# Attention into a top-1 mixture of experts: exponentials two steps behind, flips beside the sums, ranks behind them

## The chip, the core and the metric

One NeuronCore of a Trainium2 chip runs the kernel as one program. The metric is device time in microseconds (us), median of the runs shown. Five engines work side by side, each through its own queue in order: TensorE (PE, with weight loads as PEld), VectorE (DVE), ScalarE (ACT), GpSimd (POOL) and SyncE (SP, which only issues transfers here). Matmul results land in PSUM, everything else lies in SBUF.

## The reference

Attention over 8 batches, 12 heads, 448 positions and 64 features, with a tanh cap on the scores, then a router that picks one of 8 experts for each of the 3584 tokens, then that expert's two-layer network:

```python
scores = cap * np.tanh((q @ k.T / 8) / cap)
attn = softmax(scores)                 # over the keys
x = (attn @ v) -> tokens x 768
logits = x @ w_gate + modality_bias[modality_id]
e = argmax(logits); gate = softmax(logits)[e]
out[token] = gate * (relu(x @ w1[e]) @ w2[e])
```

## The kernel before

The 12 heads of a batch are 3 **units** of 4 heads, so there are 24 units `d`. A unit has 7 **steps** of 64 keys; step `n = 7 d + s` of 168 handles 64 keys against all 448 queries for the unit's 4 heads. Softmax needs no maximum, since the cap bounds the scores.

A step is this. PE makes scores: 4 matmuls (`scores`, L489) into one of two PSUM buffers `sc`. ACT takes a tanh of 128x896 into `pt` (L494). After each odd step ACT takes one exponential over the pair of steps, 128x1792 in place (L497). DVE adds the step's `pt` into the unit's `tot` (`add`, L510). PE multiplies an older step's `pt` with the values (`weigh`, L522) into the one PSUM buffer `xT`, which DVE copies out at a unit's end (`keep`, L529, "the values' copy"). In text below T(n) is the tanh of step n and E the exponential of a pair.

Everything is pinned to the order in which the loop over `n` writes it. `LAGS`, `PLAGS` say how many steps behind its scores a step's weigh stands; `BEHIND` does so for the additions. A step without a weigh is made up for by a step with two.

Every second unit, `sums2` (L556 ff.) sums over the keys for two units and multiplies the kept values with the gate weights: 8 matmuls into one PSUM bank `glog`, which DVE copies to `gl` (L567). `turn2` then flips `gl` with 4 transposes (`flip`, L552) into a bank `lt`, and DVE makes reciprocals (L580) and logits (`logits`, L603). When a batch is complete, `start_route` begins its route: a reduction (L250), the top expert, a small exponential on ACT (L269), running counts, then the **ranks**, two small matmuls (L290, L292) into a bank of their own, and row numbers (L296 to L303) by which POOL scatters the tokens into a map. `go_on` takes a route one stage further. The network of the experts (from about 306 us on) follows; it is not touched.

Of the kernel before, what the change touches and what calls it, by code (L numbers as in the profile page):

```python
# [80 lines left out]
PLAGS = (5, 5, 5, 4, 4, 4, 4)  # L81
# [4 lines left out]
class Program:  # L86
# [368 lines left out]
    def attention(self, firsts, rp, xp):  # L455
        tc, nc = self.tc, self.nc
        pe, pin, V = nc.tensor, self.pin, nc.vector
        with ExitStack() as st:
# [21 lines left out]

            def scores(n):

                d, s = divmod(n, STEPS)
                sc = ps_s.tile([128, 2, 512], F32, name="sc")
                for i in range(2):
                    kq = ring[(2 * d + i) % 4]
                    for j in range(2):
                        rows = slice(j * D, (j + 1) * D)
                        pin(pe.matmul(  # L489
                            sc[i * KB : (i + 1) * KB, j, :S], kq[rows, s * KB : (s + 1) * KB], kq[rows, S:QK],  # L490
                            start=True, stop=True,
                        ))
                slow = n // STEPS == SOON + 2 and 2 <= n % STEPS <= 5
                pin(nc.scalar.activation(weights(n), sc[:, :, :S], AF.Tanh, scale=self.isc if slow else self.iscr))  # L494
                if n % 2:
                    pt = pts[n // 2]
                    pin(nc.scalar.activation(pt, pt, AF.Exp, scale=self.cabsr))  # L497
# [33 lines left out]
            def sums(d, bank=None, copy=V.tensor_copy):  # L531
# [14 lines left out]
                gls[d] = xp.tile([128, S], F32, name="gl", bufs=2)  # L546
                pin(copy(gls[d], glog[:, :S]))

            def flip(gl, bank=None):
                bank = bank or self.ps_r.tile([128, 512], F32, name="lt", tag="small")  # L550
                for c in range(C):
                    pin(pe.transpose(bank[:CP, c * 128 : (c + 1) * 128], gl[:, c * CP : (c + 1) * CP], self.ident))  # L552
                return bank[:CP].rearrange("p (c g x) -> p c g x", c=C, g=4)

            def sums2(a, copy=V.tensor_copy):
# [10 lines left out]
                gls[a] = xp.tile([128, S], F32, name="gl", bufs=2)  # L566
                pin(copy(gls[a], glog[:, :S]))  # L567

# [7 lines left out]
            def turn2(a):  # L576

                lt = flip(gls.pop(a))
                for u in range(2):
                    pin(V.reciprocal(recs(a + u), lt[:, :, 2 * u : 2 * u + 2, GE : GE + 2]))  # L580
                    lts[a + u] = lt[:, :, 2 * u : 2 * u + 2]
# [48 lines left out]
            def start_route(b, firm=False):  # L630
                way = self.route(
                    b, lgs[b], pays[b], rp, self.ps_r, bank=(lambda: self.glog) if firm else None, firm=firm, late=firm
                )
                next(way)
                routing[:] = [way]
# [19 lines left out]
            for m in range(END):  # L655
                d, s = divmod(m, STEPS)
                due[min(m + (LAST if d == ND - 1 else PLAGS if d < PAIRED else LAGS[d % 2])[s], END)].append(m)
            added, held = 0, range(STEPS * (SOON + 2), STEPS * (SOON + 2) + 5)

            def more(n, count=0):  # L660
                nonlocal added
                while (n not in held or count > 0) and added <= n - BEHIND + (n >= END - STEPS):
# [5 lines left out]

            fetch(0)
            self.gate_weights()  # L670
            for n in range(END):
# [17 lines left out]
                if (s == 6 or s == 1) and d != SOON + 2:  # L689
                    go_on()  # L690
                if s == 4 and d % 2 and 3 <= d < PAIRED + 3:
                    turn2(d - 3)
                    go_on()
                    logits(d - 3)
                    logits(d - 2)
                if s == 4 and d % 2 == 0 and 2 <= d <= PAIRED:
                    sums2(d - 2)
                if (d, s) == (SOON + 1, 5):
                    sums(SOON)
                if s == 5 and d % 2 and 3 <= d < PAIRED + 2:  # L700
                    for u in (d - 3, d - 2):
                        if u % NU == NU - 1:
                            start_route(u // NU)
                if (d, s) == (SOON + 2, 2):
                    more(n, 2)
                for m in due[n]:
                    weigh(m)
                    if m % STEPS == STEPS - 1:
                        keep(m // STEPS)
                if s == 2 and d % NU == 2:  # L710
# [626 lines left out]
```

## Time and profile before

| | |
|---|---|
| median of 3 runs | 820.83 us (820.09 to 821.06) |
| profiled execution | 819.97 us, span of its instructions 818.4 us |
| PE busy | 803.1 us (98%) |
| DVE busy | 518.5 us (63%) |
| ACT busy | 516.0 us (63%) |
| POOL busy | 139.2 us (17%) |
| granted TensorE clock, mean | 0.998 |

A busy PE isn't a PE at its peak: the ends of matmuls are modelled, and four 64x64 matmuls run at once. In the first 300 us PE, ACT and DVE are all busy for most of the time; afterwards PE is the only one.

### The profile page before, as it was taken

The page shows a single profiled execution, that of the slowest core. Times are in us where ns is not written, and L with a number is a line of the kernel's source. Part 1 is how long each engine was busy: PE and PEld are TensorE (multiplying, and loading weights), DVE is VectorE, ACT ScalarE, POOL GpSimd, SP SyncE. Part 2 cuts the span into 40 slices and gives each one's busy share as a digit, 9 for nine tenths or more (in the row PEclk, how much of TensorE's full clock was granted, in tenths as well). Part 3 has the DMA queues.
Part 4 walks back from the last instruction along what each step waited for, and adds up shares of the span by engine and source line. Part 5 has one row for each costly group of instructions (what it writes and reads, how often), then busy time and mean ns, then how long its engine had stood idle before and what let it go on. Part 6 is the DMA issues. An engine that isn't in the chain of part 4 may idle for free. (4 is left out here: it accounts for less than half of the span.)

```text
span 818.4 us, 15444 instructions
## 1 busy us (share of the span) xinstructions
PE 803.1 (98%) x5988; PEld 608.9 (74%) x5988; DVE 518.5 (63%) x865; ACT 516.0 (63%) x655; POOL 139.2 (17%) x163
## 2 busy tenths in 40 slices
PE   7999999999999999999999999999999999999997
PEld 2333333333333348999999999999999999989996
DVE  4778888888788898764446344453544635447662
ACT  6999999999999994443444334444254443546562
POOL 2000220012021221451203113031120310111010
PEclk9999999999999999999999999999999999999999
DMA  5375536264454653977556365563665545557670
GB/s 187 116 218 194 144 131 203 74 200 147 149 181 137 189 188 89 274 233 277 208 178 230 117 216 209 189 204 135 205 230 186 200 151 183 167 190 254 219 222 29
DMA packets 57011, 148.44 MB, mean 181 GB/s; under 512 B 7758, under 2 KB 22366, under 8 KB 56928
## 3 DMA queue, kind: packets, MB, share of 16 engines
q1 hardware_dynamic: 48224, 113.34, 43.6%
q0 software_dynamic: 8560, 34.02, 11.6%
q8 instruction: 49, 0.80, 0.4%
q14 instruction: 34, 0.28, 0.1%
q10 hardware_dynamic: 144, 0.00, 0.0%
HBM read 114.44 MB, written 24.64 MB: 170 GB/s over the span
## 5 line engine op out<-in xcount | busy, mean ns | idle before, releaser
L961 PE MATMUL ph<-x,al 128*128 128x384 f32 (+2 forms) x510 | 159.9, 314 | 0.0
L1014 PE MATMUL py<-bh,hh 128*128 128x384 f32 x464 | 158.5, 342 | 0.4 <-ACT hh L972 0.3
L1014 PE MATMUL py<-bl,hh 128*128 128x384 f32 x464 | 155.6, 335 | 0.0
L1014 PE MATMUL py<-bh,hl 128*128 128x384 f32 x464 | 155.4, 335 | 0.0
L522 PE MATMUL xT<-pt,va 64*64 64x448 f32 x1344 | 151.8, 537 | 1.1 <-DVE xT L529 1.1
L494 ACT ACTIVATE pt<-sc 128x896 f32<-128x896 f32 x164 | 142.9, 906 | 11.4 <-PE sc L489 11.4
L497 ACT ACTIVATE pt<-pt 128x1792 f32<-128x1792 f32 x84 | 142.7, 1699 | 2.7
L510 DVE TENSOR_TENSOR tot<-tot,pt 128x896 f32<-128x896 f32 x118 | 127.7, 1082 | 10.8 <-ACT pt L497 6.4
L957 PE MATMUL ph<-x,ah 128*128 128x384 f32 x366 | 122.4, 334 | 0.0
L958 PE MATMUL ph<-x,ah 128*128 128x384 f32 x366 | 122.3, 334 | 0.0
L900 DVE TENSOR_TENSOR bl<-raw,bh 128x768 fp32r<-128x768 f32 x88 | 81.3, 954 | 52.6 <-ACT bh L899 52.6
L522 PEld LDWEIGHTS xT<-pt,va 64*64 64x64 f32 x1344 | 50.5, 133 | 73.7 <-issue 68.4
L1030 ACT ACTIVATE ot<-py,mt 128x384 f32<-128x384 f32 (+1 forms) x58 | 33.5, 579 | 102.6 <-PE py L1014 66.1
L972 ACT ACTIVATE hh<-ph 128x384 fp32r<-128x384 f32 x64 | 31.2, 491 | 105.7 <-PE ph L961 98.9
L961 PEld LDWEIGHTS ph<-x,al 128*128 128x128 f32 x510 | 96.0, 188 | 0.0
L900 DVE TENSOR_TENSOR al<-raw,ah 128x1024 fp32r<-128x1024 f32 x60 | 71.0, 1222 | 27.8 <-ACT ah L899 27.8
L1014 PEld LDWEIGHTS py<-bh,hh 128*128 128x128 f32 x464 | 87.1, 188 | 1.2 <-ACT hh L972 0.6
L1014 PEld LDWEIGHTS py<-bl,hh 128*128 128x128 f32 x464 | 87.2, 188 | 0.2 <-DVE bl L900 0.2
L1014 PEld LDWEIGHTS py<-bh,hl 128*128 128x128 f32 x464 | 87.1, 188 | 0.0
L899 ACT CAST bh<-raw 128x768 fp32r<-128x768 f32 x88 | 70.1, 836 | 24.2 <-DMA raw<-in_w_dram 24.0
L489 PE MATMUL sc<-kq 64*64 64x448 f32 x672 | 79.4, 547 | 3.7 <-ACT pt L494 2.6
L489 PE MATMUL sc<-kx 64*64 64x448 f32 x672 | 78.6, 540 | 0.8 <-ACT pt L494 0.8
(188 smaller groups left out, 909.6 us busy)
## 6 DMA issues: line engine op xcount, KB each, us to landing
raw<-in_w_dram SPq DMA_DIRECT2D x88, 384.0 KB, 4.5
raw<-in_w_dram SPq DMA_DIRECT2D x62, 512.0 KB, 4.1
kq<-in_kq_dram SPq DMA_DIRECT2D x24, 448.0 KB, 3.6
va<-in_v_dram SPq DMA_DIRECT2D x24, 448.0 KB, 5.5
kx<-in_kq_dram SPq DMA_DIRECT2D x24, 448.0 KB, 4.3
xd<-xs SPq DMA_DIRECT2D x32, 336.0 KB, 6.4
xr<-xg POOLq DMA_DIRECT2D x24, 384.0 KB, 3.1
mapd<-spare SPq DMA_DIRECT2D x4, 480.0 KB, 6.2
```

Source lines behind the costliest of these rows:

```text
L489: pin(pe.matmul(sc[i * KB : (i + 1) * KB, j, :S], kq[rows, s * KB : (s + 1) * KB], kq[rows, S:QK], start=True, stop=True,))
L494: pin(nc.scalar.activation(weights(n), sc[:, :, :S], AF.Tanh, scale=self.isc if slow else self.iscr))
L497: pin(nc.scalar.activation(pt, pt, AF.Exp, scale=self.cabsr))
L510: pin(V.tensor_tensor(tots[d], pt_of(n - 1) if s == 1 else tots[d], pt_of(n), op=ALU.add))
L522: pin(pe.matmul(self.xT[j * D : (j + 1) * D, i, :S], vas[d][rows, o : o + D], pt[rows, j], start=s == 0, stop=s == STEPS - 1,))
L899: keep((cast.tensor_copy if cast else self.nc.scalar.copy)(hi, raw))
L900: keep((minus or self.nc.vector).tensor_tensor(lo, raw, hi, op=ALU.subtract))
L957: keep(nc.tensor.matmul(ph[:, :w], hi[:, fs], self.x[:, k, 0, :w], start=first, stop=False))
L958: keep(nc.tensor.matmul(ph[:, :w], hi[:, fs], self.x[:, k, 1, :w], start=False, stop=False))
L961: keep(nc.tensor.matmul(ph[:, :w], lo[:, fs], self.x[:, k, 0, :w], start=False, stop=last))
L1014: nc.tensor.matmul(pys[half][:, :HALF], self.h[a][:, f, rows], self.w2s[f][c][:, cs], start=f == i == 0, stop=f == FC - 1 and i == 2,)
L1030: put = nc.scalar.mul(ot[:, half * HALF :][:, :cut], pys[half][:, :cut], mt[:, t, 1:2])
```

## The change

Five things move, all in units 0 to 19.

1. Up to step 126 (`APART`) the exponential of a pair stands behind the tanh of the next pair, not behind its own. At step 127 two exponentials follow each other. `PLAGS` grow by two steps, `CLOSER` brings units 18 and 19 back, and additions stand one step later (`BEHIND` + 1) up to step 126.
2. `sums2` moves from s = 4 to s = 6 of the even unit, which is again the step without a weigh.
3. For the pairs of units 0 to 12 (`LATER`) the flips move from s = 4 of the next odd unit to s = 6 of the even unit after, right ahead of that unit's `sums2`. They are float32r: the copy `gl` goes through a transfer on SP into a float32r tile first.
4. A route is a table of steps now. It starts in an odd unit behind the values' copy, and its ranks stand in the next even unit at s = 6, right behind the `sums2` there, in columns 448 and on of the same bank `glog`.
5. `gl` and the float32r tile have one buffer each where `gl` had two.

```diff
-PLAGS = (5, 5, 5, 4, 4, 4, 4)
+PLAGS = (7, 7, 7, 7, 6, 6, 6)
+CLOSER = ((7, 7, 6, 6, 5, 5, 5), (6, 5, 5, 5, 4, 4, 4))
+APART = STEPS * (PAIRED - 2)
+LATER = PAIRED - 8
...
                 if n % 2:
-                    pt = pts[n // 2]
-                    pin(nc.scalar.activation(pt, pt, AF.Exp, scale=self.cabsr))
+                    last = n // 2 if n > APART else n // 2 - 1
+                    while expd[0] <= last:
+                        pt = pts[expd[0]]
+                        pin(nc.scalar.activation(pt, pt, AF.Exp, scale=self.cabsr))
+                        expd[0] += 1
...
-            def flip(gl, bank=None):
+            def flip(gl, bank=None, whole=False):
                 bank = bank or self.ps_r.tile([128, 512], F32, name="lt", tag="small")
+                dst, ident = (bank.bitcast(F32R), self.identr) if whole else (bank, self.ident)
...
-                gls[a] = xp.tile([128, S], F32, name="gl", bufs=2)
+                gls[a] = xp.tile([128, S], F32, name="gl", tag="gl")
                 pin(copy(gls[a], glog[:, :S]))
+                if a <= LATER:
+                    whole = xp.tile([128, S], F32R, name="glr", tag="glr")
+                    self.last_sp = pin(nc.sync.dma_start(whole.bitcast(F32), gls[a])).ins
+                    gls[a] = whole
...
-                    b, lgs[b], pays[b], rp, self.ps_r, bank=(lambda: self.glog) if firm else None, firm=firm, late=firm
+                    b, lgs[b], pays[b], rp, self.ps_r, bank=lambda: self.glog, firm=firm, late=firm
...
-                while (n not in held or count > 0) and added <= n - BEHIND + (n >= END - STEPS):
+                while (n not in held or count > 0) and added <= n - BEHIND - (n < APART) + (n >= END - STEPS):
...
+                at = a + 5 if a <= LATER else a + 3
+                steps = ((at, 1), (at, 3), (at, 6), (at + 1, 6)) if a <= LATER else ((at, 5), (at, 6), (at + 1, 1), (at + 1, 6))
...
-                if s == 4 and d % 2 == 0 and 2 <= d <= PAIRED:
+                if s == (4 if d == PAIRED else 6) and d % 2 == 0 and 2 <= d <= PAIRED:
+                    if 0 <= d - 4 <= LATER:
+                        turn2(d - 4)
+                        logits(d - 4)
+                        logits(d - 3)
                     sums2(d - 2)
+                for at in routes.get((d, s), ()):
+                    at()
...
+                if (d, s) in starts:
+                    start_route(starts[d, s])
```

ACT at the start of the loop; the number behind `pt` is the pair's buffer. Before:

```order
L494 ACTIVATE pt_224<-sc_219 128x896
L494 ACTIVATE pt_224<-sc_226 128x896
L497 ACTIVATE pt_224<-pt_224 128x1792
L494 ACTIVATE pt_238<-sc_233 128x896
L494 ACTIVATE pt_238<-sc_240 128x896
L497 ACTIVATE pt_238<-pt_238 128x1792
```

Changed:

```order
L499 ACTIVATE pt_224<-sc_219 128x896
L499 ACTIVATE pt_224<-sc_226 128x896
L499 ACTIVATE pt_237<-sc_232 128x896
L499 ACTIVATE pt_237<-sc_239 128x896
L504 ACTIVATE pt_224<-pt_224 128x1792
L499 ACTIVATE pt_251<-sc_246 128x896
L499 ACTIVATE pt_251<-sc_253 128x896
L504 ACTIVATE pt_237<-pt_237 128x1792
```

The rhythm of two tanh and an exponential stays; the exponential now reads what was written three instructions earlier.

PE around `sums2` in unit 8. Before, with the ranks two steps behind it in their own bank:

```order
L489 MATMUL sc<-kq 64x448 x4
L561 MATMUL glog<-tot,pick_98 32x448 x4
L563 MATMUL glog<-xT,wgt 32x448 x4
L489 MATMUL sc<-kq 64x448 x4
L522 MATMUL xT<-pt,va 64x448 x4
L489 MATMUL sc<-kq 64x448 x4
L290 LDWEIGHTS tri
L290 MATMUL rank<-oh,tri 112x32
L292 LDWEIGHTS ones
L292 MATMUL rank<-before,ones 112x32
L522 MATMUL xT<-pt,va 64x448 x4
```

Changed:

```order
L494 MATMUL sc<-kq 64x448 x4
L561 MATMUL lt<-identr,glr 112x128 x4
L570 MATMUL glog<-tot,pick_98 32x448 x4
L572 MATMUL glog<-xT,wgt 32x448 x4
L293 LDWEIGHTS tri
L293 MATMUL glog<-oh,tri 112x32
L295 LDWEIGHTS ones
L295 MATMUL glog<-before,ones 112x32
L494 MATMUL sc<-kx 64x448 x4
```

Flips, sums and ranks now lie between one step's scores and the next's. In the built program the first rank matmul (L293) waits for a count of DVE's semaphore, and the instruction with that count is the copy of `glog` to `gl` (L576).

DVE at the same place of the changed kernel, from the values' copy (L537) to that copy:

```order
L537 COPY xT<-xT 128x896
L518 TENSOR_TENSOR tot<-pt 128x896
L593 RECIPROCAL pay_889<-lt 112x4x2x2 x2
L616 TENSOR_TENSOR lg<-lt,pay_889 112x4x16 x4
L253 TENSOR_REDUCE L<-lg 112x32
L576 COPY gl<-glog 128x448
```

Before, nothing stood between the values' copy and the copy of `glog`; reciprocals, logits and the reduction of the next route stood seven steps later.

## Rows read from the trace of the kernel before

**Rows 1.** Stretches: PE, PEld, DVE, ACT, POOL busy us (instructions), clock, DMA share, GB/s

```profile
160.43:185.09 24.66, 24.55 (x250) 9.21 (x246) 21.44 (x43) 23.55 (x23) 4.39 (x6) 1.00 0.55 171
```

**Rows 2.** Timeline of ACT, the first steps: start us, duration us, instruction, count

```profile
7.86 1.73 ACT L494 ACTIVATE pt<-sc 128x896 f32<-128x896 f32 x2 [4.98 <-PE sc L489]
9.61 1.70 ACT L497 ACTIVATE pt<-pt 128x1792 f32<-128x1792 f32 x1
11.22 1.71 ACT L494 ACTIVATE pt<-sc 128x896 f32<-128x896 f32 x2
12.96 1.70 ACT L497 ACTIVATE pt<-pt 128x1792 f32<-128x1792 f32 x1
...
29.67 1.70 ACT L497 ACTIVATE pt<-pt 128x1792 f32<-128x1792 f32 x1
```

**Rows 3.** Timeline of ACT, small exponential ahead of T(140)

```profile
249.89 0.21 ACT L269 ACTIVATE ex<-L 112x32 f32<-112x32 f32 x1
250.01 1.71 ACT L494 ACTIVATE pt<-sc 128x896 f32<-128x896 f32 x2
```

**Rows 4.** Waits of ACT from 20 to 300 us: in total, times, longest

```profile
ACT pt L494 <- PE sc L489: 6.8, 18, 0.6
```

**Rows 5.** Timeline of ACT behind attention: a read of PSUM, then one of SBUF

```profile
303.96 0.48 ACT L926 CAST x<-ptr 128x384 fp32r<-128x384 f32 x1
304.33 1.07 ACT L647 CAST ah<-raw 128x1024 fp32r<-128x1024 f32 x1
```

**Rows 6.** Timeline of PE around the sums of unit 12

```profile
156.07 0.93 PE L522 MATMUL xT<-pt,va 64*64 64x448 f32 x8
156.82 0.97 PE L489 MATMUL sc<-kq 64*64 64x448 f32 x8
157.73 0.96 PE L561 MATMUL glog<-tot,pick 128*32 128x448 f32 x8
158.51 0.94 PE L563 MATMUL glog<-xT,wgt 128*32 128x448 f32 x8
159.38 0.98 PE L489 MATMUL sc<-kq 64*64 64x448 f32 x8
```

**Rows 7.** Timeline of ACT around the same sums, T(86) to T(89)

```profile
155.87 1.71 ACT L494 ACTIVATE pt<-sc 128x896 f32<-128x896 f32 x2
157.60 1.70 ACT L497 ACTIVATE pt<-pt 128x1792 f32<-128x1792 f32 x1
159.21 0.90 ACT L494 ACTIVATE pt<-sc 128x896 f32<-128x896 f32 x1
160.43 0.92 ACT L494 ACTIVATE pt<-sc 128x896 f32<-128x896 f32 x1 [0.32 <-PE sc L489]
```

**Rows 8.** Timeline of PE: float32 flips of unit 13, float32r transposes of the network

```profile
169.57 0.93 PE L489 MATMUL sc<-kx 64*64 64x448 f32 x8
170.43 0.65 PE L552 MATMUL lt<-ident,gl 128*112 128x128 f32 x4
171.06 0.98 PE L489 MATMUL sc<-kx 64*64 64x448 f32 x8
...
395.76 0.37 PE L916 MATMUL ptr<-identr,xr 128*128 128x128 f32 x3
395.97 0.41 PE L1014 MATMUL py<-bh,hh 128*128 128x384 f32 x1
```

**Rows 9.** Timeline of DVE: values' copy, reciprocals, logits, reduction, copy of the sums

```profile
96.73 1.09 DVE L529 COPY xT<-xT 128x896 f32<-128x896 f32 x1 [1.15 <-PE xT L522]
98.03 0.37 DVE L580 RECIPROCAL pay<-lt 112x16 f32<-112x16 f32 x2 [0.21 <-PE lt L552]
98.33 0.61 DVE L603 TENSOR_TENSOR lg<-lt,pay 112x64 f32<-112x64 f32 x4
98.86 1.08 DVE L510 TENSOR_TENSOR tot<-pt 128x896 f32<-128x896 f32 x1
99.86 0.86 DVE L250 TENSOR_REDUCE L<-lg 112x32 f32<-112x384 f32 x1
100.76 0.19 DVE L253 TENSOR_TENSOR L<-L,bias 112x32 f32<-112x32 f32 x1
...
111.07 0.62 DVE L567 COPY gl<-glog 128x448 f32<-128x448 f32 x1 [1.05 <-PE glog L563]
```

**Rows 10.** Timeline of PE: ranks of a route, and the next weigh

```profile
161.80 0.22 PE L290 MATMUL rank<-oh,tri 112*112 112x32 bf16 x1
162.00 0.98 PE L522 MATMUL xT<-pt,va 64*64 64x448 f32 x8
```

More of the change, by code (lines that the diff above doesn't have):

```diff
@@ L479, in weights @@
                 return pts[n // 2][:, n % 2 * 2 : n % 2 * 2 + 2]
+            expd = [0]
             def scores(n):
@@ L545, in sums @@
                     ))
-                gls[d] = xp.tile([128, S], F32, name="gl", bufs=2)
+                gls[d] = xp.tile([128, S], F32, name="gl", tag="glr" if d == ND - 1 else "gl")
                 pin(copy(gls[d], glog[:, :S]))
-            def flip(gl, bank=None):
+            def flip(gl, bank=None, whole=False):
                 bank = bank or self.ps_r.tile([128, 512], F32, name="lt", tag="small")
+                dst, ident = (bank.bitcast(F32R), self.identr) if whole else (bank, self.ident)
                 for c in range(C):
-                    pin(pe.transpose(bank[:CP, c * 128 : (c + 1) * 128], gl[:, c * CP : (c + 1) * CP], self.ident))
+                    pin(pe.transpose(dst[:CP, c * 128 : (c + 1) * 128], gl[:, c * CP : (c + 1) * CP], ident))
                 return bank[:CP].rearrange("p (c g x) -> p c g x", c=C, g=4)
@@ L576, in turn2 @@
             def turn2(a):
-                lt = flip(gls.pop(a))
+                lt = flip(gls.pop(a), whole=a <= LATER)
                 for u in range(2):
@@ L656, in attention @@
                 d, s = divmod(m, STEPS)
-                due[min(m + (LAST if d == ND - 1 else PLAGS if d < PAIRED else LAGS[d % 2])[s], END)].append(m)
+                lags = LAST if d == ND - 1 else LAGS[d % 2] if d >= PAIRED else CLOSER[d % 2] if d >= PAIRED - 2 else PLAGS
+                due[min(m + lags[s], END)].append(m)
             added, held = 0, range(STEPS * (SOON + 2), STEPS * (SOON + 2) + 5)
@@ L667, in more @@
                         break
+            starts, routes = {}, {}
+            for b in range(B - 2):
+                a = (b * NU + NU - 1) // 2 * 2
+                at = a + 5 if a <= LATER else a + 3
+                steps = ((at, 1), (at, 3), (at, 6), (at + 1, 6)) if a <= LATER else ((at, 5), (at, 6), (at + 1, 1), (at + 1, 6))
+                starts[steps[0]] = b
+                for step in steps[1:]:
+                    routes.setdefault(step, []).append(go_on)
             fetch(0)
@@ L688, in attention @@
                     self.gate_bias()
-                if (s == 6 or s == 1) and d != SOON + 2:
-                    go_on()
-                if s == 4 and d % 2 and 3 <= d < PAIRED + 3:
+                if s == 4 and d % 2 and LATER + 5 <= d < PAIRED + 3:
                     turn2(d - 3)
-                    go_on()
                     logits(d - 3)
                     logits(d - 2)
-                if s == 4 and d % 2 == 0 and 2 <= d <= PAIRED:
+                if s == (4 if d == PAIRED else 6) and d % 2 == 0 and 2 <= d <= PAIRED:
[3 more added lines that the diff above has]
+                        logits(d - 3)
                     sums2(d - 2)
+                for at in routes.get((d, s), ()):
+                    at()
                 if (d, s) == (SOON + 1, 5):
                     sums(SOON)
[L700 to L703, printed above, removed]
                 if (d, s) == (SOON + 2, 2):
```

## The prediction

> **What bounds the kernel now.** I read the stretches first. In the 24.66 us from one sums block to the next, ACT is busy 23.55 us, PE 24.55, DVE 21.44, at full clock [rows 1]. PE's figure hides short waits, so I went on to ACT's timeline, where every instruction stands alone. Its cycle is tanh, tanh, exponential. From the first exponential to the seventh, 9.61 to 29.67, six cycles take 20.06 us, 3.343 each [rows 2]. T(0) starts at 7.86 [rows 2] and T(140) at 250.01 [rows 3], 242.15 us later. Seventy cycles are 234.0, and six small exponentials of the routes cost 0.12 each (249.89 to 250.01) [rows 3], 0.7 in all. So ACT sets the pace, and 7.4 us are surplus in which it was held up by PE; the list of waits names 6.8 us of such, 18 times, for scores [rows 4].
>
> How does PE hold it up? By the sums. PE can start the scores of step n only when T(n-2) has freed a buffer. In unit 12 the scores of step 88 start at 156.82, just behind the end of T(86) at about 156.78; the sums follow at 157.73, and the scores of step 89 only at 159.38, ending at 160.36 [rows 6]. T(88) starts at 159.21; T(89) could follow 0.79 later (1.71 less 0.92) at 160.00 and starts at 160.43 [rows 7]. I take this as the pattern: lay PE's items end to end from the end of T(n-2), and compare with when ACT wants T(n+1). Below, clocks start at that end.
>
> **The change part by part.**
>
> *Exponentials behind.* Today an exponential waits for the tanh just ahead: T pair at 11.22, exponential at 12.96, 1.74 later, though two tanh only fill 1.71 [rows 2]. Where neighbours on ACT don't depend on each other they overlap: an exponential and the tanh behind it by 9.61 + 1.70 - 11.22 = 0.09 [rows 2]; a read of PSUM followed by one of SBUF, as here, 0.48 against 0.37, 0.11 [rows 5]. So tanh to exponential goes from 0.95 to 0.92 less 0.11, 0.81: 0.14 saved. Exponentials 0 to 63 gain it: **-9.0 us**. By 0.09 it would be -7.7, by an overlap of 0.14 -10.9. The Trainium skill, ScalarE: Activation LUTs, in "What ACT_TABLE_LOAD costs", has back-to-back ACTIVATEs overlap by about 93 ns; by that alone the term would be an estimated -7.9, and the exponential's row agrees with it. The cycle becomes 3.20, and ACT wants T(n+1) 3.08 after the end of T(n-2).
>
> At the start four tanh stand in a row and only two score buffers are free: T(2) needs scores that can't start before T(0) ends, about 8.77, and take 0.98 [rows 2, 6], so it starts at 9.87 where ACT could take it at 9.44: **+0.4**.
>
> *Sums at s = 6, flips ahead of them, ranks behind.* The surplus of today goes, **-7.4**; in its place come the new blocks. PE's items: scores to sums 0.91, sums to the second half 0.78, second half to the next scores 0.87, scores 0.98 to their end, 0.07 until the tanh starts, 0.05 at the front [rows 6, 7]. That is 3.66 for unit 2, which has no flips: 0.57 late (today's 0.43 with a shorter cycle). Flips: in float32 they cost 171.06 - 170.43 = 0.63. Three float32r transposes take 0.21, so four take 0.28 [rows 8]; with the change of shape behind them (0.91 less the 0.75 of plain scores, 0.16 [rows 6]) 0.44, and the way from scores to flips is 0.86 [rows 8]. A block with flips then ends at 4.04, 0.96 late: units 4, 6, 12.
>
> With ranks PE has a new wait. The first rank matmul waits for DVE's copy of the same bank, and the next scores are queued behind it. The sums end 0.94 after their second half starts [rows 6], at 3.07; copy 0.06 and 0.62 [rows 9]; 0.05 to PE, 0.20 for the ranks [rows 10]; scores and tanh 1.05. That is 5.05, 1.96 late, if DVE is ready: units 10 and 16. In units 8 and 14 DVE still has the next route's reduction in front: values' copy from about 0.05, 1.08; addition 1.00; reciprocals 0.30; logits 0.53; reduction 0.90 [rows 9], so the copy starts at 3.86 rather than 3.13, and the tanh is 2.65 late. Unit 18 has ranks without flips (0.44 less) and today's exponentials, by which ACT wants T(n+1) only at 3.22: 5.05 - 0.44 + 0.05 - 3.22, some 1.42 late (the 0.05 for the shape change at the front). Together 0.57 + 3 x 0.96 + 2 x 1.96 + 2 x 2.65 + 1.42 = **+14.1**. The Trainium skill, PSUM — Partial Sum Buffer, in "PSUM bank collisions raise a hardware error", wants two engines kept apart in one bank and quadrant even at other columns; so this wait can't be had away as long as the ranks lie in that bank, and it speaks against the place. No run here shows a collision.
>
> *Larger lags.* A step with two weighs stands at s = 3 now. From a PE that is level with ACT, three items of 0.75 (156.82 - 156.07 [rows 6]) and the scores to their tanh end at 3.36 against 3.08: 0.27 late in the eight odd units 3 to 17, less 0.12 in four of them that have a small exponential there: **+1.7**. In unit 17 the float32 flips come on top of it, **+0.5**. Units 18 and 19 catch up two steps with two more double weighs, each behind a PE that the ranks have already made late by some 0.1 more: 0.4 each by the same items, **+0.8**.
>
> *Hidden at nothing.* The transfers of `gl` (7 on SP) stand in front of the next unit's loads, which have a unit's 12 us; the float32r tile is read 24 us later. Additions a step later still end before their buffers come round, three steps of slack. The values' copy ends at about 1.15 and the second half of the sums needs it at 2.2. DVE's work in total is unchanged. From T(140) on the order is today's, so what is won or lost there arrives at the end.
>
> **Sum.** -9.0 + 0.4 - 7.4 + 14.1 + 1.7 + 0.5 + 0.8 = **+1.1 us**. The profiled execution of 819.97 would become 821.1; the median stands 0.86 above it, so 821.9.
>
> **The rivals.**
>
> *The rank wait is hidden* (faster). If the copy of `glog` is finished when PE comes to the ranks, these cost their 0.20 alone: 1.16 in units 8, 10, 14 and 16 and about 0.7 in unit 18, so 2 x 1.49 + 2 x 0.80 + 0.7 = 5.3 less: 816.6. For it: ACT may then also gain the larger overlap. Against it: the copy can only start at the sums' end, and PE has nothing between.
>
> *DVE comes later to the copy* (slower). The five rank blocks are paid to the full by anything that DVE does first, 5 us for each us. It decides from 0.11 us per block on, since I stand at +1.1 and 0.2% is 1.64. For it: DVE is at 21.44 of 24.66 us [rows 1], additions now wait for later exponentials, and route work lies loose between pinned rows. Against: with route work gone by s = 4 the queue should be level at the block. At 0.6 us each, 3 more: 824.9.
>
> *The exponential doesn't overlap* with a tanh ahead that it doesn't need (slower). Then only the gap of 0.03 goes, 64 x 0.11 = 7.0 dearer: 828.9. Against it are all independent neighbours on ACT [rows 2, 5].
>
> **How the numbers follow.** 0.2% of 820.8 is 1.64 us, about what a measurement of this kernel can tell from no change, so "same" is 819.2 to 822.5. My forecast has a chance of 0.48, 0.42 of it within that and 0.06 above; the hidden wait 0.18 (0.16 faster, 0.02 same); the late DVE 0.29 (0.28 slower, 0.01 same); no overlap 0.05. Faster 0.16, same 0.45, slower 0.39. The range reaches from the forecast less the larger overlap and shorter blocks to the late DVE: 818.0 to 825.0, leaving out the full hidden wait and the missing overlap. The forecast's own range, by 0.09 to 0.14 of overlap and 0.2 per rank block, is 819.5 to 824.0.
>
> **What would show it.** In the changed profile, exponentials 0 to 63 should start about 0.8 behind the tanh ahead, and ACT's free cycle should be 3.20. ACT's waits for scores should grow from 6.8 to some 14 to 17 us, the longest at steps 63, 77, 105 and 119 (units 8, 10, 14, 16), at 2 to 2.6 us, with PE's first rank matmul waiting for L576. If these waits are under 1 us, the hidden wait holds; if they pass 3 us, DVE was late; if exponentials still start 0.94 behind, the overlap was wrong. T(140) should start about 1 us later than 250.01, and everything behind it should be shifted by the same.

## The result, and the profile after

The changed kernel takes 831.16 us (828.03 to 832.42, 4 runs) against 820.58 of the kernel before beside it: 1.0123 times as long, 95% interval 1.0092 to 1.0155. A later repetition gave 1.0140 (1.0122 to 1.0158). The prediction, 821.9 with a range to 825.0, was wrong. The profiled execution took 832.26, its span 830.7.

Where did the time go? The first view to read is the table of stretches, cut at tanh 0, 126, 140 and 167 (the last). Columns: stretch; its length, then busy us (instructions) of PE, PEld, DVE, ACT, POOL; granted clock; DMA share; GB/s. The kernel before:

```profile
7.86:225.60 217.74, 213.36 (x2164) 79.74 (x2160) 173.60 (x286) 211.40 (x194) 20.05 (x31) 1.00 0.51 162
225.60:250.01 24.41, 24.30 (x250) 9.05 (x246) 21.28 (x43) 23.55 (x23) 4.40 (x6) 1.00 0.55 170
250.01:297.40 47.39, 46.30 (x473) 17.28 (x469) 41.99 (x82) 45.01 (x42) 14.80 (x17) 1.00 0.51 152
297.40:818.40 521.00, 512.92 (x3091) 499.94 (x3083) 279.03 (x445) 234.60 (x397) 96.19 (x94) 1.00 0.58 193
```

The changed kernel, cut at the same four tanh:

```profile
8.53:228.91 220.38, 207.86 (x2128) 78.78 (x2120) 169.73 (x284) 203.24 (x193) 21.73 (x30) 1.00 0.52 165
228.91:259.54 30.63, 27.73 (x266) 10.23 (x270) 22.86 (x38) 25.21 (x25) 4.40 (x6) 0.94 0.51 144
259.54:308.04 48.50, 47.41 (x489) 17.96 (x485) 43.04 (x85) 45.20 (x42) 14.67 (x17) 1.00 0.51 150
308.04:830.70 522.66, 513.67 (x3091) 500.07 (x3083) 279.62 (x445) 235.06 (x397) 97.06 (x94) 1.00 0.58 193
```

The two spans differ by 12.3 us. 6.2 of these lie in the fourteen steps from 126 to 140, and only there the clock isn't full. 2.6 more come in the 126 steps ahead, although ACT is busy for 8 us less there. But the cut at tanh 126 puts one exponential, 1.6 us, into the second stretch that stood in the first before. Counted where it was, the second loses 4.6 and the first 4.2: the many steps ahead weigh nearly as much as the one place with the low clock. The third stretch adds 1.1, the start 0.7. The last one's 1.7 belongs to that execution: the repetition's has 520.8 there.

Was ScalarE's part of the change as foreseen? Timeline of ACT at the start of the changed kernel (start, duration, instruction, count):

```profile
15.35 1.71 ACT L504 ACTIVATE pt<-pt 128x1792 f32<-128x1792 f32 x1
16.93 1.73 ACT L499 ACTIVATE pt<-sc 128x896 f32<-128x896 f32 x2
18.53 1.72 ACT L504 ACTIVATE pt<-pt 128x1792 f32<-128x1792 f32 x1
```

The free cycle is 18.53 - 15.35 = 3.18, where [rows 2] have 3.343. So it was. Who is waited for shows in the list of waits between 20 and 300 us (engine and line, whom it waited for; in total, times, longest):

```profile
ACT pt L499 <- PE sc L494: 24.4, 24, 3.3
...
PE glog L293 <- DVE gl L576: 5.4, 5, 1.6
PE xT L530 <- DVE xT L537: 4.5, 3, 2.9
PE sc L494 <- ACT pt L499: 3.9, 9, 0.5
```

ACT waits 24.4 us for scores; [rows 4] have 6.8. Behind a part of that stand two waits of PE for DVE: five times the first rank matmul for the copy of the sums, as foreseen, and three times a weigh for a values' copy, the longest, 2.91 us, the first weigh of unit 18 for the copy of unit 17. The last row is the other way round: PE waits for ACT too, nine times. Timeline around the longest wait for a copy:

```profile
225.04 0.85 DVE L253 TENSOR_REDUCE L<-lg 112x32 f32<-112x384 f32 x1
...
226.12 0.93 PE L494 MATMUL sc<-kq 64*64 64x448 f32 x8
...
228.15 0.56 DVE L286 TENSOR_TENSOR before<-before,oh 112x8 bf16<-112x8 bf16 x3
...
228.82 1.08 DVE L537 COPY xT<-xT 128x896 f32<-128x896 f32 x1
...
229.96 1.77 PE L530 MATMUL xT<-pt,va 64*64 64x448 f32 x8 [2.91 <-DVE xT L537]
...
231.51 1.56 PE L494 MATMUL sc<-kq 64*64 64x448 f32 x8
...
233.15 0.92 ACT L499 ACTIVATE pt<-sc 128x896 f32<-128x896 f32 x1 [3.33 <-PE sc L494]
```

A whole route, from the reduction (L253) to the running counts (L286), stands in DVE's queue ahead of the values' copy (L537). PE's last scores end at 227.05, and then it has nothing to do until that copy ends. When it goes on, eight matmuls take 1.77 us where they took 0.93. The stretches say why (columns as above):

```profile
228.00:230.00 2.00, 0.04 (x4) 0.04 (x4) 1.83 (x7) 1.82 (x3) 0.00 (x0) 0.84 0.98 351
230.00:231.00 1.00, 1.00 (x8) 0.50 (x12) 1.00 (x2) 0.00 (x0) 0.00 (x0) 0.50 1.01 398
...
233.00:234.00 1.00, 1.00 (x16) 0.33 (x12) 1.00 (x3) 0.85 (x2) 0.00 (x0) 1.00 0.00 0
```

The granted clock is 0.50, the 1.2 GHz level, behind the idle time, and back at full by 233.

One thing has to be known for the numbers below: in three of the five sittings the kernel before took 820.3 to 820.7 us and in two 829.2 and 830.5, and ratios don't carry over from the ones to the others, so that pairs of units are compared in the traces where a comparison crosses them.

### The profile page after: what moved, and what is told of

The parts are those of the page before. It is cut to its first block, busy times and chain, and to the rows that moved or that the text cites. A ratio compares the mean times of both kernels' runs of the same rounds, so it can differ in the third digit from the quotient of the medians.

```text
span 830.7 us, 15462 instructions
## 1 busy us (share of the span) xinstructions
PE 803.6 (97%) x5988; PEld 610.1 (73%) x5988; DVE 518.4 (62%) x865; ACT 510.2 (61%) x655; POOL 142.3 (17%) x163
## 5 line engine op out<-in xcount | busy, mean ns | idle before, releaser
L499 ACT ACTIVATE pt<-sc 128x896 f32<-128x896 f32 x164 | 145.3, 921 | 30.4 <-PE sc L494 29.8
L313 POOL DMA_INDIRECT mapd<-pay,pos x32 | 36.1, 1129 | 267.8 <-DVE pos L306 220.9
```

What stands on the lines that cost most here:

```text
L313: put = nc.gpsimd.indirect_dma_start(self.mapd, bass.IndirectOffsetOnAxis(ap=pos[:, c : c + 1], axis=0), pay[:, c, :], None, bounds_check= ...
```

## The experiments

There were eighteen runs, in five sittings (1 to 4, 5 to 8, 9 to 12, 13 to 16, 17 and 18). A **pair** is two units from tanh to tanh, without a rank unless told.

**1. The route held behind the copy.** Batch 4's route instructions on DVE are pinned where they are written, which is behind the values' copy.

```diff
+class Held:
+    def __init__(self, pin, engine):
+        self.pin, self.engine = pin, engine
+
+    def __getattr__(self, name):
+        op = getattr(self.engine, name)
+        return lambda *a, **k: self.pin(op(*a, **k))
...
+        vec = Held(self.pin, nc.vector) if isinstance(b, int) and b == 4 else nc.vector
-        nc.vector.tensor_reduce(L, lg.rearrange("p c h e -> p c e h"), axis=AX.X, op=ALU.add)
+        vec.tensor_reduce(L, lg.rearrange("p c h e -> p c e h"), axis=AX.X, op=ALU.add)
...
```

> The changed kernel, but the route of batch 4 (it starts in unit 17) is held in written order on VectorE, so that unit 17's values' copy comes ahead of all route work. Theory A: the copy came late (228.82 us) because a whole route had been put in front of it; TensorE then waited 2.91 us with the next values' product, its clock fell to half for 3.4 us, and T(127) came 3.33 us late. Then T(127) loses at most 0.3 us here, no half clock shows at that place, and the time is 3.3 to 4.5 us under the changed kernel's 831.2: 826.7 to 827.9. Rival B: VectorE is simply full there, and the work only moves: the wait comes back at the ranks of unit 18, and the time stays within 1 us of 831.

827.27 us, 1.0075 (1.0054 to 1.0095): 3.9 less by the medians. From tanh 0 to 140 its trace has 247.85 us, the changed kernel's 251.01: 3.2. In its timeline the copy starts at 225.28, and PE weighs at once:

```profile
225.28 1.09 DVE L547 COPY xT<-xT 128x896 f32<-128x896 f32 x1 [0.17 <-PE xT L540]
...
226.54 0.93 PE L540 MATMUL xT<-pt,va 64*64 64x448 f32 x8
```

The clock stays full there. The route in front of the copy is a cause, worth 3 to 4 us.

**2. Ranks a step later.**

```diff
-                steps = ((at, 1), (at, 3), (at, 6), (at + 1, 6)) if a <= LATER else ((at, 5), (at, 6), (at + 1, 1), (at + 1, 6))
+                steps = ((at, 1), (at, 3), (at, 6), (at + 2, 0)) if a <= LATER else ((at, 5), (at, 6), (at + 1, 1), (at + 2 * (b == 4) + (b != 4), 6 * (b != 4)))
```

> The changed kernel with the rank matmuls one step later, behind the scores of the odd unit's first step, when VectorE's copy of the sums is done. Theory A: the rank wait in the block costs what the trace shows beside a block without ranks (idle of ScalarE 3.01 and 2.16 us against 1.18; 1.29 in unit 18 against some 0.5). Then these five waits fall to 1.2 and 0.5, 6.4 us in all, less some 0.3 us a time for the ranks in their new place: about 5 us under the changed kernel, 826. Rival B: TensorE sets the pace, and what is taken from one wait comes back at the next scores: under 2 us.

826.50, 1.0069 (1.0049 to 1.009): 4.7 less by the medians, 3.8 from tanh 0 to 140. Timeline in unit 8 and 9:

```profile
112.34 0.98 PE L494 MATMUL sc<-kx 64*64 64x448 f32 x8
113.39 0.92 ACT L499 ACTIVATE pt<-sc 128x896 f32<-128x896 f32 x1 [1.18 <-PE sc L494]
114.03 0.18 PE L293 MATMUL glog<-oh,tri 112*112 112x32 bf16 x1 [0.71 <-DVE gl L576]
...
117.49 0.92 ACT L499 ACTIVATE pt<-sc 128x896 f32<-128x896 f32 x1 [0.59 <-PE sc L494]
```

Scores now go ahead of the ranks, and tanh 63 waits 1.18 rather than 3.01; part of it comes back two steps on (0.59). The wait at step 127 stayed, with its low clock.

**3. Exponentials behind their own pair again.**

```diff
-                    last = n // 2 if n > APART else n // 2 - 1
+                    last = n // 2
```

> The changed kernel with each exponential behind its own pair's tanh again, all else as changed. Theory A: ScalarE sets the pace, and the 0.16 us per pair that the trace shows (cycle 3.18 against 3.34) are a gain of 64 x 0.16 = 10 us: this is slower by 8 to 10 us, 840. Rival B: with the blocks as they are TensorE sets the pace, and the exponentials only made ScalarE wait longer: at most 2 us slower or none, 831 to 833.

833.06, 1.0147 (1.0127 to 1.0168): only 1.9 more, and the two intervals overlap, so the time alone doesn't tell it from nothing. The traces do: a pair takes 24.45 us with them there and 24.13 in the changed kernel. The 0.14 us a cycle that ACT was to save, 1.0 in a pair, show as 0.32.

**4. Both mends together** (1 and 2).

> The route of batch 4 held and the ranks one step later, together. If both waits are causes of their own the gains add up: 831.2 - 4 - 5 = 822, with T(140) about 252 us after 259.5. If they share one cause (VectorE full) it is no better than the better of the two alone.

825.21, 1.0057 (1.0039 to 1.0074), and 1.0048 (1.003 to 1.0066) when repeated (below). By the medians the gains don't add up to 8.6. But from tanh 0 to 140 this trace has 244.54 us, 6.5 less than the changed kernel's, and 3.2 and 3.8 of the mends alone are 7.0: nearly the sum, so they are two causes. More than 4 us are left beside the kernel before, though PE waits only 1.4 us for the copy of the sums now, rather than 5.4, and no weigh waits longer than 1.1.

**5. Flips apart.** The flips and logits go back to a step without the sums, the odd unit's one without a weigh; all these routes start a unit earlier, held in order as in run 1, with ranks in a bank of their own. Since these move together, only a pair without ranks prices the flips' place.

```diff
-LATER = PAIRED - 8
+LATER = PAIRED - 6
...
-                    b, lgs[b], pays[b], rp, self.ps_r, bank=lambda: self.glog, firm=firm, late=firm
+                    b, lgs[b], pays[b], rp, self.ps_r, bank=(lambda: self.glog) if firm else None, firm=firm, late=firm
-                at = a + 5 if a <= LATER else a + 3
-                steps = ((at, 1), (at, 3), (at, 6), (at + 1, 6)) if a <= LATER else ((at, 5), (at, 6), (at + 1, 1), (at + 1, 6))
+                at = a + 4 if a <= LATER else a + 3
+                steps = ((at, 1), (at, 3), (at, 6), (at + 1, 2)) if a <= LATER else ((at, 5), (at, 6), (at + 1, 1), (at + 1, 6))
-                    if 0 <= d - 4 <= LATER:
-                        turn2(d - 4)
-                        logits(d - 4)
-                        logits(d - 3)
                     sums2(d - 2)
+                if s == 6 and d % 2 and 0 <= d - 3 <= LATER:
+                    turn2(d - 3)
+                    logits(d - 3)
+                    logits(d - 2)
```

> Built on the changed kernel. The sums stay alone in the even unit's last step; the flips as float32r and the logits move to the last step of the odd unit before it, which has no weighing; every route before unit 19 is held on VectorE in the order it is written, starts one unit earlier, and its ranks go into a bank of their own behind steps that leave time for VectorE, so that no rank waits for the flips' copy in the same bank and no values' copy queues behind a route. Theory: the new lateness comes from what was put together in one step (sums, flips, ranks in one bank) and from the route in front of the copy, not from the amount of work. Then the wait of 2.91 us in front of the values' transposes at step 127 and the half clock behind it are gone, the waits of 1.60 and 0.75 for the flips' copy too, and a pair of units takes 23.7 us as units 2 and 3 take without flips; T of step 140 comes 3 to 4.5 us before that of the kernel before, and the time is 817 to 819. Rival: TensorE's work per pair of units is what sets the pace and it is unchanged by where the flips stand; then pairs stay at 24.1 and the time is that of the kernel with both mends, 824 to 826.

824.97 beside 829.21: 0.994 (0.9923 to 0.9958). The pair is 23.69 us rather than 24.13, as expected. But this is one of the two sittings in which the kernel before took 829 to 831, so the ratio was measured again in runs 11 and 16.

**6. Both mends, with the exponentials at their own pair.** Edit 3 in kernel 4.

> The kernel with both mends (batch 4's route held behind the copy, ranks a step later; 825.2) and the exponential put back behind its own pair of tanh. It prices the exponentials' move where the long waits are gone. If TensorE sets the pace in the paired units, as the run with the exponentials put back in the changed kernel said (+1.9), it costs 1 to 3 us here: 826 to 828. If ScalarE sets it once the waits are gone, the whole 64 times 0.14 to 0.16, 9 to 10 us, comes back: 834 to 835.

833.87 beside 829.21: 1.0054 (1.0035 to 1.0073). The ratio can't be set against kernel 4's, which ran elsewhere. Its pair is 24.46, 0.33 more than kernel 4's 24.13: 3.0 us over nine pairs. So ScalarE doesn't set the pace alone without the long waits either.

**7. Flips in fp32.** No transfer on SP, no float32r tile, and two buffers for `gl` again.

```diff
-                if a <= LATER:
+                if False:
...
-                lt = flip(gls.pop(a), whole=a <= LATER)
+                lt = flip(gls.pop(a), whole=False)
```

> The changed kernel with the flips in fp32 in units 0 to 14 too, and without the transfer on SP's queue that makes the float32r copy of the logits. It prices the type alone: eight transposes of fp32 take about 0.2 us more of TensorE's time per flip than of float32r by the rows of the kernel before. Theory: TensorE is what ScalarE waits for there, so eight flips cost 8 times 0.2 to 0.4, and the time is 832.5 to 834. Rival: the wait is for the flips' copy on VectorE and behind the sums' copy and the transfer, not for the transposes; then the transfer's going gives as much or more, and the time is 829 to 831.5.

836.43 beside 829.21: 1.0087 (1.0061 to 1.0112). In the trace the pair is 24.27, 0.14 more than the changed kernel's. Tanh 0 to 126 take 222.39 us rather than 220.38, 0.4 of it one late start of the kind shown under run 8: some 0.2 for each of the seven flips, the low end of what was expected. The whole time doesn't tell, for want of the changed kernel in that sitting.

**8. Flips apart, other lags at the end.** `CLOSER = ((7, 7, 6, 6, 5, 5, 4), (5, 5, 5, 4, 4, 4, 4))`.

> The kernel with the flips apart and one more edit: in the last two paired units the additions' lags are chosen so that no step from 139 to 141 weighs two pairs. The changed kernel, with two pairs weighed at steps 139 and 141, had waits of ScalarE of 0.56 and 0.31 us at steps 141 and 143 that the kernel before did not have. Theory: these come back whole, 0.6 to 1 us less than the kernel with the flips apart. Rival: the double weighs move to step 138, where the values' copy of unit 18 is due, and the wait moves with them: within 0.3 us of it.

825.91, 0.9942 (0.9922 to 0.9962): the same as kernel 5's within the intervals, as the rival said. Its trace shows what that sitting has that the others don't:

```profile
98.57 0.98 PE L504 MATMUL sc<-kq 64*64 64x448 f32 x8
99.77 0.98 PE L540 MATMUL xT<-pt,va 64*64 64x448 f32 x8 [0.22 <-issue]
100.79 0.92 ACT L509 ACTIVATE pt<-sc 128x896 f32<-128x896 f32 x1 [2.27 <-PE sc L504]
```

The scores end at 99.55, and the tanh that waits for them starts 1.24 later, where 0.07 is usual. Each trace of these two sittings has four to six tanh that start over 0.3 us behind their scores, most of them 0.6 to 1.7; those of the others have none. Their cause isn't known.

**9. The exponentials' move alone,** put into the kernel before, with its own lags.

```diff
+                    last = n // 2 if n > APART else n // 2 - 1
+                    while expd[0] <= last:
+                        pt = pts[expd[0]]
+                        pin(nc.scalar.activation(pt, pt, AF.Exp, scale=self.cabsr))
+                        expd[0] += 1
```

> The kernel before with one part of the change alone: each exponential behind the next two tanh, up to step 126. Lags, additions, flips and ranks are those of before. Theory: a pair of an even step m is weighed four steps later in most of a unit, and its exponential now runs on ScalarE only behind the tanh of step m+3, so TensorE, in order, stands at that weighing until the exponential's 1.7 us are over; scores queued behind it come about 1 us late for the tanh, some four times in a pair of units. That is 15 to 30 us more than before, 835 to 850: the part cannot be had without the longer lags. Rival: the scores ahead of the weighing are enough, ScalarE's shorter cycle shows, and the time is 812 to 816.

860.35 beside 830.49: 1.0361 (1.0338 to 1.0384), 29.9 us more, as expected. The list of PE's waits names it:

```profile
PE xT L528 <- ACT pt L502: 30.6, 34, 1.7
```

Weighs stand and wait for exponentials. The move needs the longer lags, and with these comes the way back to the short ones in units 18 and 19, with two more steps of two weighs.

**10. Flips apart, exponentials at their own pair.** Edit 3 in kernel 5, with kernel 5 again beside it (11).

> The kernel with the flips apart and the exponential put back behind its own pair of tanh. Theory: with the flips apart TensorE has room, ScalarE sets the pace, and the exponentials' place is worth its 0.14 to 0.16 us for each of 64 pairs, so this is 8 to 10 us slower than the kernel with the flips apart on the same chip, and some 4 us slower than before. Rival: TensorE still sets the pace as in the changed kernel, where putting them back cost 1.9: then it is 1 to 3 us slower.

> The kernel with the flips apart once more, with more rounds and beside the kernel with the exponentials put back. Expected: 0.992 to 0.997 of the kernel before, as in its first run; the rival, that its lead over the kernel before belonged to that chip alone, would give 0.998 to 1.002.

829.10 (0.9982, 0.9966 to 0.9998) and 826.02 (0.994, 0.9921 to 0.9958): 3.1 us apart, just over the rival's 1 to 3. One pair of each in the table of stretches, first exponentials at their own pair, then behind:

```profile
31.17:55.19 24.02, 23.79 (x252) 9.04 (x248) 17.66 (x23) 23.38 (x22) 0.00 (x0) 1.00 0.52 168
```

```profile
29.16:52.85 23.69, 23.69 (x248) 9.15 (x244) 17.75 (x23) 22.69 (x23) 0.00 (x0) 1.00 0.54 171
```

In the second PE is busy 23.69 of 23.69 us, ACT 22.69. How much of that is work? From start to start in run 16's timeline of this pair a block of scores or of a weigh takes 0.75 us, the sums 1.8 and the flips 0.66 on top. 28 blocks and these are 23.5, an estimate: PE has some 0.2 us to spare, and a faster ScalarE can win no more than that. But PE's work isn't the whole reason. Units 2 and 3 of the changed kernel have no flips, and their pair is as long:

```profile
30.00:53.69 23.69, 23.27 (x244) 8.79 (x240) 17.75 (x18) 22.68 (x22) 0.00 (x0) 1.00 0.54 171
```

PE stands there for 0.42 us at one place, waiting for a tanh:

```profile
51.47 0.98 PE L494 MATMUL sc<-kq 64*64 64x448 f32 x8 [0.42 <-ACT pt L499]
```

In both pairs ACT waits 0.75 us behind the sums and 0.26 behind the step with two weighs. So each of the two waits for the other through the two score buffers, and flips put apart fill the time in which PE stood.

**12. Additions back,** four steps behind, in the changed kernel.

```diff
-                while (n not in held or count > 0) and added <= n - BEHIND - (n < APART) + (n >= END - STEPS):
+                while (n not in held or count > 0) and added <= n - BEHIND + (n >= END - STEPS):
```

> The changed kernel with the additions of exponentials put back to four steps behind, as before. The prediction held the later additions at nothing. Theory: within 1 us of the changed kernel, ratio 1.011 to 1.0135. Rival: an addition four steps behind stands on VectorE until the later exponential is over, the copies queued behind it come later by 0.5 to 1 us in each unit, and the time is 3 to 8 us more than the changed kernel, ratio 1.016 to 1.022; the step later would then be a needed part of the change.

841.46 beside 830.49: 1.0135 (1.0109 to 1.016), which taken alone would say "nothing". The trace says otherwise. Tanh 0 to 126 take 8.0 us more than the changed kernel's 220.38:

```profile
8.31:236.69 228.38, 209.67 (x2128) 78.88 (x2120) 172.01 (x285) 204.32 (x194) 21.28 (x31) 0.99 0.51 160
```

0.9 of these are a late start. Pairs take 24.50 instead of 24.13, those with ranks up to 2.7 more, and in unit 8:

```profile
113.06 1.09 DVE L518 TENSOR_TENSOR tot<-tot,pt 128x896 f32<-128x896 f32 x1 [0.69 <-ACT pt L504]
...
115.75 0.61 DVE L576 COPY gl<-glog 128x448 f32<-128x448 f32 x1
...
118.47 0.92 ACT L499 ACTIVATE pt<-sc 128x896 f32<-128x896 f32 x1 [4.63 <-PE sc L494]
```

An addition waits for its exponential in front of the copy of the sums, and tanh 63 waits 4.63 us rather than 3.01. The later additions are a needed part of the change, worth some 7 us up to tanh 126 by these traces. What they are worth in the whole time stays open, for want of the changed kernel in that sitting.

**13 to 16. Before, changed, both mends and flips apart in one sitting,** since ratios had turned out not to carry over.

> The kernel before, for its trace on the chip on which the flips apart ran (829 to 830 us there against 821 on the first chip). If the 8 to 9 us lie in waits that have nothing to do with the change, a pair of units without a route's work still takes 24.0 to 24.2 us there, and the surplus stands in a few places: units 19 to 23 and single late starts of ScalarE. If the paired units are slower there throughout, pairs take 24.5 or more.

> The changed kernel beside the kernel before, with both mends and flips apart on one chip. If its ratio does not depend on the chip it is 1.0123 again (1.0092 to 1.0155), and then the additions put back (1.0135) cost nothing and the flips as fp32 (1.0087) are 3 us better. If the chip takes part of it away it is 1.006 to 1.009, and then the additions put back cost 4 us, as their pairs of 24.50 instead of 24.13 say (nine pairs, 3.4), and the type of the flips is worth little.

> Both mends (batch 4's route held behind the copy, ranks a step later) beside the kernel with the flips apart. On the first chip 1.0057 of the kernel before. Its step 140 came 242.7 to 244.5 us behind step 0; the flips apart have 240.7. If the flips' place is worth that difference, it is 4 to 9 us slower than the flips apart (0.994), 1.000 to 1.006 of the kernel before.

> The flips apart beside these three. Expected 0.992 to 0.997 of the kernel before whatever the chip; the rival, that on a chip with fewer late starts the lead goes, 0.998 to 1.002.

Beside 820.42: before 820.93 (1.0005, 0.9994 to 1.0016), changed 831.40 (1.0140, 1.0122 to 1.0158), both mends 824.48 (1.0048, 1.003 to 1.0066), flips apart 820.16 (0.9998, 0.9989 to 1.0008). So the flips apart take back all that the change lost, 11.2 us, and win nothing over the kernel before: their 0.994 belonged to the sittings with late starts. Run 13 was on the chip of runs 5 to 8, where the kernel before had taken 829.2, and it has no late start: it was the sitting, not the chip. The stretches of the flips apart, a pair with ranks, then tanh 0 to 140 and 140 to 167:

```profile
101.35:125.41 24.06, 24.06 (x250) 9.22 (x246) 21.60 (x43) 22.73 (x24) 5.26 (x6) 1.00 0.37 126
8.44:247.68 239.24, 235.23 (x2402) 88.88 (x2398) 194.22 (x324) 228.06 (x216) 26.75 (x35) 1.00 0.55 172
247.68:296.89 49.21, 47.79 (x481) 17.59 (x477) 43.66 (x86) 45.10 (x43) 15.06 (x19) 1.00 0.49 146
```

The kernel before, in the same sitting, has

```profile
8.76:250.95 242.19, 237.69 (x2410) 88.82 (x2406) 194.43 (x324) 234.95 (x217) 23.64 (x36) 1.00 0.50 162
250.95:298.36 47.41, 46.32 (x473) 17.30 (x469) 42.03 (x82) 45.02 (x42) 15.01 (x17) 1.00 0.51 151
```

2.95 us are won up to tanh 140 and 1.8 given back behind it. The largest piece is tanh 145, which waits 2.08 us instead of 0.58. It stands behind the sums of step 144, whose weight loads wait for DVE: 1.1 us for an addition, 0.8 for the values' copy.

**17 and 18. The way back to short lags spread over three units; and ranks two steps later besides.**

```diff
-CLOSER = ((7, 7, 6, 6, 5, 5, 5), (6, 5, 5, 5, 4, 4, 4))
+CLOSER = ((7, 7, 7, 6, 6, 5, 5), (6, 6, 5, 5, 5, 4, 4), (5, 5, 5, 4, 4, 4, 4))
...
```

```diff
-                steps = ((at, 1), (at, 3), (at, 6), (at + 1, 2)) if a <= LATER else ((at, 5), (at, 6), (at + 1, 1), (at + 1, 6))
+                steps = ((at, 1), (at, 3), (at, 6), (at + 1, 4)) if a <= LATER else ((at, 5), (at, 6), (at + 1, 1), (at + 1, 6))
```

> The flips apart, with the additions' lags of units 17 to 19 chosen so that the way back from lag 7 to lag 5 is spread over three units (pairs weighed together at steps 126 to 128, 129, 133 and 135 rather than at 134, 139 and 141) and the last paired unit has those of the kernel before. The flips apart had ScalarE wait 2.07 us at step 145, 0.59 at 137 and 0.20 at 143 where the kernel before had 0.58, 0 and 0. Theory: TensorE, behind after the double weighs of steps 139 and 141, brings the sums of step 144 late; with the spread these go, 1.5 to 2.3 us: 818 to 819, 0.997 to 0.998 of the kernel before. Rival: the sums wait for the additions on VectorE, behind the held route of batch 5, whatever the lags: within 0.4 us of the flips apart, 1.000.

> The same with the ranks of the first five batches two steps later, after the step of unit 7 (9, 13, 15 too) that weighs two pairs. In the flips apart a pair of units with ranks takes 24.06 us, one without 23.69, and ScalarE waits 0.62 two steps behind the ranks. Theory: the ranks' matmuls fall together with the double weigh; two steps later they find TensorE level, and the pairs take 23.69 to 23.8: 1.3 to 1.9 us less than the kernel with the lags spread. Rival: the ranks cost TensorE their time wherever they stand: within 0.4 us of it.

819.97 (0.9991, 0.9983 to 1.0000) and 820.03 (0.9994, 0.9985 to 1.0003) beside 820.31. With the lags spread, tanh 140 to 167 take 48.16 us instead of 49.21, but unit 19 starts 1.06 late instead of 0.31. Tanh 145 still waits 1.32, and the loads of its sums still wait for DVE (0.63 and 0.84 us), which was the rival. With the ranks later their pair goes from 24.06 to

```profile
100.47:124.36 23.89, 23.89 (x250) 9.23 (x246) 21.72 (x43) 22.84 (x23) 5.67 (x7) 1.00 0.39 127
```

half of what was expected, and PE is busy all through it. The steps from 126 to 140 give most of the gain back: 28.06 us instead of 27.47. No version is clearly faster than the kernel before. That TensorE's own work is what is left next everywhere is argued from its busy share and not shown.

## Why the prediction was wrong

**What was right.** The exponential's place on ACT: the cycle is 3.18, foreseen 3.20. The rival without overlap was wrong. The Trainium skill, ScalarE: Activation LUTs, in "What ACT_TABLE_LOAD costs", has back-to-back ACTIVATEs overlap by about 93 ns; here an exponential and the tanh behind it overlap by 15.35 + 1.71 - 16.93 = 0.13, a little more. The rank wait of L293 for L576 was named, at the right units and in the right order of sizes. "From T(140) on" the shift came through to the end, with 1.1 us more from unit 20.

**The step that failed outright** stands under "Hidden at nothing": "the values' copy ends at about 1.15". That is so where the sums stand, but in unit 17 batch 4's route begins in the step ahead, and its rows lie loose on DVE in front of the copy. The prediction had seen that "route work lies loose between pinned rows", but as a rival for the copy of the sums, not for that of the values. 3.33 us of waiting, most of it for DVE and the rest at half clock; run 1 gives 3.2 to 3.9 for it.

**The step that was mis-sized** is the assumption under all the block terms, that PE comes level with ACT to the block ("from the end of T(n-2)", 0.05 at the front). In unit 8:

```profile
108.31 1.84 ACT L499 ACTIVATE pt<-sc 128x896 f32<-128x896 f32 x2
...
109.74 0.93 PE L494 MATMUL sc<-kq 64*64 64x448 f32 x8
109.99 1.09 DVE L537 COPY xT<-xT 128x896 f32<-128x896 f32 x1 [2.47 <-PE xT L530]
...
110.61 0.50 PE L561 MATMUL lt<-identr,glr 128*112 128x128 f32 x4
...
113.69 0.61 DVE L576 COPY gl<-glog 128x448 f32<-128x448 f32 x1
...
114.35 0.18 PE L293 MATMUL glog<-oh,tri 112*112 112x32 bf16 x1 [1.60 <-DVE gl L576]
...
115.56 0.92 ACT L499 ACTIVATE pt<-sc 128x896 f32<-128x896 f32 x1 [3.01 <-PE sc L494]
```

Tanh 60 ends at about 109.23, and the scores of step 62 start at 109.74: PE is 0.5 behind. The values' copy waits for PE's last weigh and starts at 0.76, 0.7 later than the 0.05 of the prediction. By the prediction's own sign a wait over 3 us meant that DVE was late; here it is 3.01, and DVE was waiting for PE. The step with two weighs at s = 3 had put PE behind, and with items of 0.75 each against a cycle of 3.18 for four of them it makes up only 0.18 a cycle. The waits measured against those foreseen (to a wait, add some 0.11 of overlap that a waiting tanh loses, which the foreseen figures contain):

| place | foreseen | ACT's wait |
|---|---|---|
| unit 2 | 0.57 | 0.75 |
| units 4, 6, 12 | 0.96 | 1.18 each |
| units 10, 16 | 1.96 | 2.16 each |
| units 8, 14 | 2.65 | 3.01 each |
| unit 18 | 1.42 | 1.29 |
| double weighs in odd units | 0.27 less small exponentials | 0.26 in four |
| unit 17, fp32 flips | 0.5 | 0.47 |
| units 18, 19, double weighs | 0.4 each | 0.31 each |
| step 127, values' copy | 0 | 3.33 |
| unit 20, double weighs of steps 139, 141 | 0 | 0.56 and 0.31 |

With the lost overlap the blocks come to 16.9 instead of 14.1, 2.8 more. Step 127 adds 3.4, unit 20 1.1. The three are 7.3 of the 9.3 us between forecast and median; 1.5 more lie up to tanh 140. The prediction counted the steps with two weighs in odd units alone, but the even ones have one at s = 3 too: in units 2 to 16 the tanh of s = 5 starts 0.93 us behind the one ahead instead of 0.79, 1.1 in all. The list of waits leaves gaps as short as these out. The rest can't be assigned.

**What lay under both.** "So ACT sets the pace" was half of it. PE's 24.55 busy us of 24.66 [rows 1] were put down as hiding short waits; run 11's pair shows PE busy for 23.69, some 23.5 of it work. ACT's shorter cycle would be 7 x 3.2 = 22.4 in a pair. The sum never held that against PE's own items over a pair, and so counted -9.0 and -7.4 as gains that the new blocks only reduce. Even where PE never waits (flips apart) the pair falls just from 24.0 or 24.1 to 23.69. The exponentials' move is worth 0.32 a pair by run 3, 0.33 by run 6 and by runs 10 and 11: a third of the 1.0 that -9.0 has for a pair.

"Additions a step later" stood at nothing, and no late addition shows in the changed kernel; run 12 shows that the change even needs it. The chance given to a late DVE, 0.29, was the nearest of the rivals, with the wrong copy.

## What to carry to other kernels

Before counting a saving on the engine that seems to set the pace, add up the other engine's own items over the same stretch in the new order: that sum is a floor, and it needs no wait to show. Two engines that hand buffers to each other can stay above both floors, as the pair without flips does. When work without a fixed place meets a queue whose copies others wait for, look at each copy that another engine needs, not only at the one that the change puts to use. And a step with doubled work leaves its engine behind for several steps, so the next block doesn't begin level.

## What the runs showed of the hardware

The clock: after 2.91 us without work TensorE ran on at 0.50 granted, and in the repetition longer than here:

```profile
229.00:230.00 1.00, 0.08 (x4) 0.08 (x8) 0.97 (x2) 0.77 (x1) 0.00 (x0) 0.59 0.98 384
...
234.00:236.00 2.00, 2.00 (x16) 0.54 (x12) 0.78 (x4) 2.00 (x3) 0.00 (x0) 0.50 0.00 0
```

After waits of 1.60 it did not fall. So a wait of that length cost its own time and then more: the next eight matmuls took 1.77 us instead of 0.93. Tanh 126 to 140 took 31.17 us in the repetition and 30.63 in the run with the shorter half clock, so the longer one cost some 0.5 more. The Trainium skill, TensorE: Matmul & The Clock Gate, in "What's actually happening", has the clock gated by how busy PE has lately been; these rows agree.

Instructions on ACT were longer in the changed kernel. Mean duration of a tanh over the first 126 steps, before and then changed (busy us, mean ns; idle ahead, and for whom):

```profile
L494 ACT ACTIVATE pt<-sc 128x896 f32<-128x896 f32 x126 | 109.7, 906 | 9.3 <-PE sc L489 9.3
```

```profile
L499 ACT ACTIVATE pt<-sc 128x896 f32<-128x896 f32 x126 | 111.8, 926 | 22.8 <-PE sc L494 22.2
```

A tanh is 20 ns longer where more of them overlap their neighbours; that the overlap is the reason is not shown. And a ratio measured in one sitting need not hold in another: the flips apart had 0.994 twice and 0.9998 in the third.
